# Layer-norm tiles moved to ScalarE in stages, and one set of weight sums moved behind a product's outputs, in a fused attention and gated-MLP kernel

## Chip, cores and metric

The kernel runs on one core of one Trainium2 chip. The metric is the device time of one execution in microseconds (us). A run is given as the median of several executions; the profile is of one execution, and its span is some 2 us shorter than its time (779.9 against 781.72 us for the kernel before).

Engine names: TensorE (PE in the profile; its weight loads are PEld), VectorE (DVE), ScalarE (ACT), GpSimd (POOL), SyncE (SP), which issues most of the DMAs here.

## The reference, cut to what matters

```python
def _layernorm(x, axis=-1, eps=1e-5):
    m = jnp.mean(x, axis=axis, keepdims=True)
    v = jnp.var(x, axis=axis, keepdims=True)
    return (x - m) / jnp.sqrt(v + eps)
...
    h = x + _A_ref(_layernorm(x, axis=-1), A_wqkv, A_wo)     # local dilated attention, 32 heads, window 8
    h2 = h + _B_ref(_layernorm(h, axis=-1), B_w_gate, B_w_up, B_w_down)   # (x Wg * x Wu) Wd
    return h2
```

x is 2048 rows of 1024 numbers in bfloat16. There are two layer norms, one ahead of attention ("first") and one ahead of the MLP ("second").

## The kernel before

The 2048 rows are done in four chunks of 512, each of four tiles of 128 rows. A normalized tile is transposed by a DMA into `lnT`, the moving operand of the next product. Each engine is given its instructions in the order in which the Python code emits them, and in the traces it runs them in that order: in the kernel before, VectorE stood 4.44 us before a weight sum (L661) although the emptying of a bank, emitted behind it (L792), could have run (the products in both banks of `ex` were done by about 505.3, the sum began at 510.42). A bank is one of the eight buffers that the kernel's pool `psum` holds (`bufs=8`), into which TensorE writes its products; the program has another engine empty it (evict the product) before TensorE uses it again, and TensorE waits for that: 3.2 us for L792 on the page of before.

Attention is VectorE work. A small scheduler, `Background`, emits its pieces between TensorE's product groups. Each group gives VectorE a credit of time and each piece takes from it:

```python
    def step(self, us):                 # called once per product group, GROUP_US = 1.73
        self.now += us
        self.credit = min(self.credit + us * self.rate, 4.0)
        while self.credit > 0:
            item = next((i for i in self.items if i[0] <= self.now), None)
            ...
                got = next(item[1])     # emits one piece, returns its estimated time
            ...
```

The output projection of a chunk with its second layer norm, and what follows it for chunk 0:

```python
    def wo_ln2(c):
        ...
        def norm(t):
            ln = normalize(hs[t], mv4, rs4, t)                     # VectorE
            nc.sync.dma_start_transpose(lnT[:, :, bass.ts(t, 128)], ln[:])
        for t in range(4):
            for hf in range(2):
                ... # 8 matmuls, then VectorE adds the product to hs[t]
                if hf == 1:
                    stats(hs[t], mv4, t)                           # VectorE
                    rstd_of(mv4, rs4, t, t + 1)                    # ScalarE, two tiny ones
                    bg.spend(1.5)
                elif t > 0:
                    norm(t - 1)
                    bg.spend(0.55)
                bg.spend(0.7)
                bg.step(GROUP_US)
        norm(3)
        retire(2)              # frees two weight tiles, SyncE issues the next two loads of 1 MB
        return lnT, hs
...
    nxt = wo_ln2(0)                      # product groups 0 to 7
    qkv(3, range(4, 6), last=True)       # product groups 8 to 15; each block of 4 frees a weight tile
    start_attention(3)
    lnT2, hs = nxt
    hT = ffn1(0, lnT2)                   # its first gate product reads all four tiles of lnT
```

Much later, the outputs of a product of chunk 1, with the weight sums of the next stage's first pair in between (a pair is a slice of the gate and up weights that is worked on together; that stage multiplies sums of blocks of the weights and of the normalized rows, here `weight_sums` and `activation_sums`):

```python
    sub([dn["kx"], dn["vx"]], dn["21"], dn["11"])
    weight_sums(0, nc.vector)            # waits for ScalarE's scaled weights, then 4 sums on VectorE
    retire(2)
    for q in range(2):
        dprod(ex[q], q, EF["21"], fcells(dn["12"]), False)
        ... result(1, hs1[2 + q], 2 + q, 1, ex[q], dn["inv"], et)   # VectorE empties bank ex[q]
    retire(1)
    activation_sums(l2, l3, dn["px"])
    for q in range(2):
        dprod(ey[q], q, EF["12"], fcells(dn["22"]), False)
        ...
    for q in range(2):
        dprod(ex[q], q, EF["22"], fcells([dn["kx"], dn["vx"]]), False)  # needs bank ex[q] empty
        ...
```

## Time and profile before

| | |
|---|---|
| time, median (lowest to highest of 4) | 784.56 us (784.07 to 785.24) |
| the profiled execution | 781.72 us, span 779.9 us |
| TensorE busy | 766.8 us |
| VectorE busy | 614.9 us |
| ScalarE busy | 473.5 us |

How to read it: TensorE is busy 766.8 of 779.9 us, at a mean granted clock of 0.999, and its instructions are in program order, so what can be won is its idle time. The busy time of the others counts where TensorE waits for them, as in the 3.2 us for VectorE's L792. The lines follow in the prediction.

### The profile page before, as it was taken

The numbers are of one execution on the slowest core, as the hardware profiler recorded it, in microseconds if no ns is written. First come the engines' busy times: TensorE is split into PE (matmuls) and PEld (weight loads), VectorE is DVE, ScalarE is ACT, GpSimd is POOL, SyncE is SP. The second block draws the span as 40 slices with busy tenths as digits, with TensorE's granted clock in tenths as the row PEclk, the third lists the DMA queues.
The fourth block names the chain that finished last, engine by engine and source line by source line (L and its number), as shares of the span: only waits on it lengthen the run. The fifth ranks groups of instructions, "written<-read, shape, count | busy, mean of one in ns | idle before, by whom it ended". The sixth has DMA issues, their size and how long they took to land.

```text
span 779.9 us, 10436 instructions
## 1 busy us (share of the span) xinstructions
PE 766.8 (98%) x3648; PEld 355.0 (46%) x3707; DVE 614.9 (79%) x805; ACT 473.5 (61%) x1028; POOL 142.4 (18%) x152
## 2 busy tenths in 40 slices
PE   8999999999999999999999999989999999999997
PEld 6544444444444444444444444434444444444444
DVE  6629999999899998999979989975553444579862
ACT  5627445313576652966769799836677677788240
POOL 0000000010000200002000001008778677600000
PEclk9999999999999999999999999999999999999999
DMA  8999693896955868858555492824332323730001
GB/s 272 260 236 209 169 274 90 262 274 173 341 174 186 297 215 234 270 189 270 195 163 195 133 313 75 183 74 110 106 99 64 108 67 97 255 123 28 1 27 55
DMA packets 181605, 133.86 MB, mean 172 GB/s; under 512 B 79024, under 2 KB 174384, under 8 KB 179504
## 3 DMA queue, kind: packets, MB, share of 16 engines
q1 hardware_dynamic: 177968, 111.17, 50.1%
q0 software_dynamic: 3584, 22.02, 8.1%
q8 instruction: 29, 0.48, 0.3%
q14 instruction: 24, 0.20, 0.1%
HBM read 104.86 MB, written 22.02 MB: 163 GB/s over the span
## 4 chain that ended last, share of the span: by engine, by line
PE 88%; DVE 9%; ACT 1%; issue 1%; DMA 1%; SPq 0%; DVEq 0%
PE ps L392 20%; PE pu L392 12%; PE pg L392 12%; PE dx L787 6%; PE pz L680 6%; PE acc L626 6%; PE py L680 6%; PE px L680 6%; PE wo L513 4%; PE pv L680 3%; PE dy L787 3%; DVE h L834 1%; PE ps L355 1%; PE ex L787 1%; DVE prodx L780 1%
## 5 line engine op out<-in xcount | busy, mean ns | idle before, releaser
L392 PE MATMUL ps<-lnT,w_qkv 128*128 128x512 bf16 x721 | 158.9, 379 | 0.8
L392 PEld LDWEIGHTS <-w_qkv 128*128 128x128 bf16 x736 | 71.9, 98 | 85.9
L392 PE MATMUL pu<-lnT,w_wu 128*128 128x512 bf16 x438 | 105.1, 379 | 0.6
L392 PE MATMUL pg<-lnT,w_wg 128*128 128x512 bf16 x440 | 105.1, 379 | 0.4
L306 ACT CAST sg<-ps 128x512 bf16<-128x512 f32 x96 | 54.8, 590 | 54.4 <-PE ps L392 51.1
L475 DVE TENSOR_TENSOR pv<-vD,at 128x4096 bf16<-128x4096 bf16 x32 | 72.5, 2287 | 0.3
L432 DVE TENSOR_TENSOR prod<-qD,kD 128x4096 bf16<-128x4096 bf16 x32 | 72.3, 2284 | 0.1
L680 PEld LDWEIGHTS <-sw 128*128 128x128 f16 x448 | 43.8, 98 | 53.2 <-issue 0.4
L392 PEld LDWEIGHTS <-w_wg 128*128 128x128 bf16 x448 | 43.8, 98 | 52.9
L392 PEld LDWEIGHTS <-w_wu 128*128 128x128 bf16 x448 | 43.8, 98 | 52.9
L596 ACT CAST us<-pu 128x512 bf16<-128x512 f32 x56 | 33.2, 593 | 41.1 <-PE pu L392 38.7
L680 PE MATMUL px<-lnT,ws 128*128 128x512 bf16 x212 | 53.1, 379 | 0.6
L680 PEld LDWEIGHTS <-ws 128*128 128x128 f16 x336 | 32.9, 98 | 39.6
L626 PE MATMUL acc<-w_wd,gs 128*128 128x512 bf16 x219 | 48.2, 379 | 0.3
L487 POOL DMA_DIRECT2D od<-oD x4 | 2.2, 544 | 252.3 <-DVE oD L485 162.5
L661 POOL TENSOR_TENSOR sw<-ws 128x512 f16<-128x512 f16 x26 | 30.0, 1154 | 87.6 <-PE py L680 80.4
L591 ACT CAST gs<-pg 128x512 bf16<-128x512 f32 x56 | 32.9, 587 | 11.4 <-PE pg L392 9.3
L185 ACT ACTIVATE rs<-mv,eps 128x1 f32<-128x1 f32 (+1 forms) x25 | 7.4, 297 | 50.3 <-DVE mv L182 47.1
L434 DVE TENSOR_TENSOR prod<-prod 128x4096 bf16<-128x4096 bf16 x16 | 36.6, 2288 | 0.3
L541 ACT ACTIVATE junkd<-w_wd 128x512 bf16<-128x512 bf16 x56 | 34.3, 613 | 0.0
L626 PEld LDWEIGHTS <-gs 128*128 128x128 bf16 x224 | 21.9, 98 | 26.4
L697 ACT COPY py<-px 128x512 f32<-128x512 f32 x28 | 16.0, 570 | 29.6 <-PE px L680 29.6
(304 smaller groups left out, 1398.0 us busy)
## 6 DMA issues: line engine op xcount, KB each, us to landing
w_wg<-in_B_w_gate_dram SPq DMA_DIRECT2D x14, 1024.0 KB, 6.6
w_wu<-in_B_w_up_dram SPq DMA_DIRECT2D x14, 1024.0 KB, 5.3
w_wd<-in_B_w_down_dram SPq DMA_DIRECT2D x8, 896.0 KB, 7.4
w_pair<-in_B_w_gate_dram SPq DMA_DIRECT2D x14, 512.0 KB, 4.0
w_pair<-in_B_w_up_dram SPq DMA_DIRECT2D x14, 512.0 KB, 5.2
w_wo<-in_A_wo_dram SPq DMA_DIRECT2D x6, 1024.0 KB, 8.4
w_qkv<-in_A_wqkv_dram SPq DMA_DIRECT2D x5, 1024.0 KB, 9.1
kd<-sg SPq DMA_DIRECT2D x32, 144.0 KB, 2.9
```

The lines of the kernel that those rows point to most:

```text
L306: nc.scalar.copy(sg[:, HB:HB + TC], ps[:])
L392: nc.tensor.matmul(ps[:], lhsT=wt[:, ko, bass.ts(j, 128)], rhs=rhs[:, ko, :], start=(ko == 0), stop=(ko == KO - 1))
L432: nc.vector.tensor_tensor(prod[:, j], qD[:], kD[:, :, o:o + SUB], ALU.mult)
L434: nc.vector.tensor_tensor(prod[:, :, 0:16], prod[:, :, 0:16], prod[:, :, 16:32], ALU.add)
L475: nc.vector.tensor_tensor(pv[:, j], vD[:, :, o:o + SUB], at[:, w, None, :].to_broadcast((128, DH, SUB)), ALU.mult)
L513: nc.tensor.matmul(ps[:], lhsT=oTs[c][:, kk, t, :], rhs=wts["wo", c, hf][:, kk, :], start=(kk == 0), stop=(kk == KO - 1))
L541: nc.scalar.activation(junk, src, ACTF.Abs, accum_out=self.l1[:, k:k + 1])
L591: nc.scalar.copy(gs[:], pg[:])
L596: nc.scalar.copy(us[:], pu[:])
L626: nc.tensor.matmul(acc[t][:], lhsT=hT[f][:, bass.ts(t, 128)], rhs=wts["wd", c, hf, b][:, j, :], start=(f == 0), stop=(f == NF - 1))
L680: nc.tensor.matmul(ps[:], lhsT=lhs[:, ko, :], rhs=rhs[:, ko, :], start=(fresh and ko == 0), stop=(ko == 3), skip_group_check=not fresh)
L787: nc.tensor.matmul(ps[:, bass.ds(lo, n)], lhsT=lhs[k][:, bass.ts(q, 128)], rhs=rhs[k][:, bass.ds(lo, n)], start=(fresh and k == 0), stop=( ...
```

## The change

Its intent: VectorE looks full in the first half of the program (busy 19.05 of the 20 us from 180 to 200), so twelve layer-norm tiles are taken from it and done on ScalarE alone, in three stages per tile, one stage per product group. Less important: the absolute sums of the down weights are taken two blocks at a time, and pair 0's weight sums go behind the outputs that they held up.

```diff
     def step(self, us):
         self.now += us
+        if self.rows:
+            next(self.rows[0], None) is None and self.rows.pop(0)
...
+    def scalar_rows(src, lnT, t, name):
+        ...
+        nc.scalar.activation(junk[:], src[:], ACTF.Copy, accum_out=total)
+        yield True
+        nc.scalar.activation(nmean, total, ACTF.Copy, scale=-1.0 / D)
+        ...
+        nc.scalar.activation(junk[:], src[:], ACTF.Square, bias=nmean, accum_out=squares)
+        yield True
+        nc.scalar.activation(rstd, squares, ACTF.Ln, bias=eps[:], scale=1.0 / D)
+        nc.scalar.activation(rstd, rstd, ACTF.Exp, scale=-0.5)
+        nc.scalar.activation(shift, nmean, ACTF.Copy, scale=rstd)
+        ...
+        nc.scalar.activation(ln[:], src[:], ACTF.Identity, bias=shift, scale=rstd)
+        nc.sync.dma_start_transpose(lnT[:, :, bass.ts(t, 128)], ln[:])
+        yield True
...
                 if hf == 1:
-                    stats(hs[t], mv4, t)
-                    rstd_of(mv4, rs4, t, t + 1)
-                    bg.spend(1.5)
-                elif t > 0:
-                    norm(t - 1)
-                    bg.spend(0.55)
+                    bg.rows.append(scalar_rows(hs[t], lnT, t, f"2_{c}_{t}"))
                 bg.spend(0.7)
                 bg.step(GROUP_US)
-        norm(3)
         retire(2)
...
-    bg.add(norm_gen(norm1[3]), bg.now, first=True)
+    bg.rows += [scalar_rows(xtiles[3][t], lnTs[3], t, f"1_3_{t}") for t in range(4)]
...
     lnT2, hs = nxt
+    bg.finish_rows()
     hT = ffn1(0, lnT2)
...
-                if c == 0:
+                if c == 0 and j % 2 == 0:
                     abs_sum_down(hf, b, j)
...
     sub([dn["kx"], dn["vx"]], dn["21"], dn["11"])
-    weight_sums(0, nc.vector)
...
     activation_sums(l2, l3, dn["px"])
+    weight_sums(0, nc.vector)
```

More of the change, by code (lines that the diff above doesn't have):

```diff
@@ L45, in __init__ @@
         self.rate = 1.0
+        self.rows = []
     def add(self, gen, ready=0.0, first=False):
@@ L67, in step, with finish_rows @@
                 self.items.remove(item)
+    def finish_rows(self):
+        for gen in self.rows:
+            for _ in gen:
+                pass
+        self.rows = []
     def finish(self, gen):
@@ L206 @@
     lnTs = {}
+    def scalar_rows(src, lnT, t, name):
+        sm = small.tile([128, 5], F32, tag="am", name="am" + name)
+        total, nmean, squares, rstd, shift = (sm[:, i:i + 1] for i in range(5))
+        junk = lnp.tile([128, D], BF, tag="ln", name="jm" + name)
+        nc.scalar.activation(junk[:], src[:], ACTF.Copy, accum_out=total)
+        yield True
+        nc.scalar.activation(nmean, total, ACTF.Copy, scale=-1.0 / D)
+        junk = lnp.tile([128, D], BF, tag="ln", name="jv" + name)
+        nc.scalar.activation(junk[:], src[:], ACTF.Square, bias=nmean, accum_out=squares)
[3 more added lines that the diff above has]
+        nc.scalar.activation(shift, nmean, ACTF.Copy, scale=rstd)
+        ln = lnp.tile([128, D], BF, tag="ln", name="ln" + name)
+        nc.scalar.activation(ln[:], src[:], ACTF.Identity, bias=shift, scale=rstd)
+        nc.sync.dma_start_transpose(lnT[:, :, bass.ts(t, 128)], ln[:])
+        yield True
     xtiles = {}
@@ L252, in rows_gen @@
                 yield 0.45
-    def stats_gen(n):
-        for t in range(4):
-            n.stat(t)
-            yield 1.5
-    def norm_gen(n):
-        for t in range(4):
-            n.norm(t)
-            n.transpose(t)
-            yield 0.55
     x0 = [hp.tile([128, D], BF, tag="h", name=f"x0_{t}") for t in range(4)]
@@ L381 @@
     xtiles[2] = load_x(2, "x", nc.sync)
-    norm1 = {c: Norm1(c) for c in (1, 2, 3)}
+    norm1 = {c: Norm1(c) for c in (1, 2)}
     bg.add(rows_gen(norm1[1], True))
@@ L502, in wo_ln2 @@
         hs = hss[c]
-        mv4, rs4 = ln_tiles(f"2_{c}")
-        def norm(t):
-            ln = normalize(hs[t], mv4, rs4, t)
-            nc.sync.dma_start_transpose(lnT[:, :, bass.ts(t, 128)], ln[:])
         for t in range(4):
@@ L560, in total @@
             self.s, self.inv = sb[:].bitcast(F32), ib[:].bitcast(F32)
-    scale_gu, scale_d, scale_h = Scale("gu", 56), Scale("d", 56), Scale("h", 56)
+    scale_gu, scale_d, scale_h = Scale("gu", 56), Scale("d", 32), Scale("h", 56)
     scale_h1 = Scale("h1", 28)
@@ L570, in abs_sum_down @@
     def abs_sum_down(hf, b, j):
-        junk = lnp.tile([128, 512], BF, tag="ln", name=f"junkd{hf}_{b}_{j}")
-        scale_d.add(28 * hf + 7 * b + j, wts["wd", 0, hf, b][:, j, :], junk[:])
+        n = min(2, 7 - j)
+        junk = lnp.tile([128, n, 512], BF, tag="ln", name=f"junkd{hf}_{b}_{j}")
+        scale_d.add(16 * hf + 4 * b + j // 2, wts["wd", 0, hf, b][:, j:j + n, :], junk[:])
     def abs_sum_h(n, k, ht):
@@ L735 @@
     pump(6)
-    bg.add(stats_gen(norm1[3]), bg.now + 6.0)
     start_attention(0)
@@ L740 @@
     load_v(0)
-    bg.add(norm_gen(norm1[3]), bg.now, first=True)
+    lnTs[3] = lnTp.tile([128, KO, TC], BF, tag="lnT", name="lnT1_3")
+    bg.rows += [scalar_rows(xtiles[3][t], lnTs[3], t, f"1_3_{t}") for t in range(4)]
     qkv(1, range(4, 6))
@@ L760 @@
     lnT2, hs = nxt
+    bg.finish_rows()
     def f16(ap):
```

## The prediction

The sum at the end of the forecast came to 792.6 us. One of its terms, for matmuls that run slower after so long a wait, rested on no trace and is cut, there and in rival (a); the terms that are left add up to 790.9 (rival (a): 787.6). "Cold clock", and "goes cold" in an expectation below, are words for such slow matmuls: the trace of the kernel before did not show them (its 3.18 us gap left the granted clock at 1.00). The paragraph ahead of "Part 1": 1.06, 1.15 and 1.24 in it are us for 1024 columns, and "both" means bias and scale from pointers.

> **What bounds the kernel now.** I read the page first, then the busy time by stretches of 20 us, then who waited for whom on TensorE (PE), then the timeline of the three places that the change touches.
>
> ```profile
> PE 766.8 (98%) x3648; PEld 355.0 (46%) x3707; DVE 614.9 (79%) x805; ACT 473.5 (61%) x1028; POOL 142.4 (18%) x152
> ...
> 180.00:200.00 20.00, 19.89 (x93) 9.00 (x94) 19.05 (x23) 6.50 (x21) 1.08 (x2) 1.00 0.80 217
> ...
> 500.00:520.00 20.00, 16.82 (x79) 7.58 (x78) 15.24 (x26) 9.68 (x8) 0.00 (x0) 1.00 0.60 119
> ...
> PE ex L787 <- DVE h L792: 3.2, 1, 3.2
> ```
>
> The columns of the two stretches are length, then busy time of PE, weight load, VectorE (DVE), ScalarE (ACT) and GpSimd, then the granted clock. TensorE is busy 766.8 of 779.9 us, so 13.1 us are idle. A full stretch shows 19.89 of 20. Only three stretches fall clearly below that: the start (17.57), the end (15.97) and 500 to 520 (16.82). The change touches neither the start nor the end. So at most about 3.3 us can be won, in one place, and any new wait of TensorE is lost time in full.
>
> The one gap, from the timeline:
>
> ```profile
> 503.96 2.02 DVE L780 TENSOR_TENSOR vx<-w_dn,w_dn 128x3584 f16<-128x3584 f16 x1
> ...
> 506.69 3.69 ACT L654 ACTIVATE ws<-w_pair,sbgu 128x4096 f16<-128x4096 bf16 x1
> ...
> 510.42 0.69 DVE L661 TENSOR_TENSOR sw<-ws 128x1024 f16<-128x1024 f16 x1 [4.44 <-ACT ws L654]
> ...
> 513.75 0.75 DVE L792 SCALAR_TENSOR_TENSOR h<-ex,inv_h1d,et 128x512 bf16<-128x512 f32 x1
> ...
> 514.56 1.67 PE L787 MATMUL ex<-kx,gs 128*128 128x512 f16 x7 [3.18 <-DVE h L792]
> ```
>
> Columns: start, duration, engine, line; in brackets the idle time before it and who ended it. VectorE stood 4.44 us before the weight sums of pair 0 (L661), waiting for ScalarE's scaled weights, then did the four sums. Only then did it empty bank ex[0], for which TensorE had stood since 511.38.
>
> The layer norms, at the change-over from qkv to the first gate product:
>
> ```profile
> 185.85 0.55 DVE L190 TENSOR_SCALAR ln<-h,mv,rs 128x1024 bf16<-128x1024 bf16 x1 [0.60 <-ACT rs L186]
> ...
> 191.13 1.89 PE L392 MATMUL pg<-lnT,w_wg 128*128 128x512 bf16 x8
> 191.33 0.59 ACT L306 CAST sg<-ps 128x512 bf16<-128x512 f32 x1 [1.04 <-PE ps L392]
> 191.81 0.21 ACT L309 COPY sg<-halo 128x16 bf16<-128x16 bf16 x1
> ```
>
> The last tile of chunk 0's second norm is normalized by 186.4. Its transpose (3.1 us from issue to landing here) lands around 190, and the first gate product starts at 191.13 without a wait. The slack is only about a microsecond.
>
> [...] 1.06 (L850, a Copy with a sum), 1.15 (L857, Square with a bias) and 1.24 (L869, Identity with both). [...] ScalarE stood 9.6 us at an exponential (L452), and evictions queued up behind such waits follow each other at 0.58 us. [...] the 3.18 us gap left the granted clock at 1.00.
>
> **Part 1, the norm tiles.** A tile on VectorE costs two statistics and an aggregate (1.45 us) and the normalization (0.55), 2.0 in all. Twelve tiles take 24 us off VectorE, which held nobody up there, so this wins nothing by itself. On ScalarE a tile becomes three stages. Stage 1: Copy with sum, 1.06 + 0.19 for reading the accumulator, about 1.2. Stage 2: a small Copy and Square with sum, about 1.5. Stage 3: Ln 0.30, Exp 0.20, a small Copy 0.20 and Identity 1.24, about 1.95. That is 4.65 per tile, 56 us for twelve tiles against 12 × 0.5 = 6 us of small instructions removed. With the saving of part 2 ScalarE then holds about 515 of 780 us and is not the bound.
>
> What decides is when a stage enters ScalarE's queue: one call per product group. A tile needs **four** calls, because the call that finds the generator ended is also spent. Number the groups from the output projection of chunk 0: 0 to 7 are that projection, 8 to 15 are qkv of chunk 3, blocks 4 and 5. Tile t is queued at group 2t+1. So tile 0 gets its stages after groups 1 to 3 (4 drops it), tile 1 after 5 to 7, tile 2 after 9 to 11 and **tile 3 after 13, 14 and 15**. Group 15 is the last before the gate product, which reads all four tiles. Stage 3 of tile 3 stands behind group 15's own eviction, and TensorE has nothing else to do. The later call that finishes leftovers finds nothing left.
>
> Floor of this wait: group 15 ends at 191.13, eviction and halo until 192.0, stage 3 until 193.95, transpose landed at 197.05. That is **5.9 us** of TensorE.
>
> Is ScalarE on time? Chunk 1's exponential stands in the same queue. I replayed the credit counting on paper. Before, it comes after the first gate group; with the norms no longer spending VectorE credit, it comes after group 10, ahead of tile 3. It needs VectorE's maxima. VectorE's lead: before, it stood until 53.85 for chunk 3's x and began attention at 59.47. The keys land at about 51.3 (issued 42.47, 8.8 to land), so it now starts 8 us earlier, and 1.9 us of normalizations also go: 10 us ahead. It then reaches the first addition at about 164.3 rather than 172.99, and follows TensorE. Adding up its items from 165.4 (eight additions of 0.65, products 2.28 each, tree sums, maxima 2.6), the maxima end at about 186.7. ScalarE from there: exponential 1.06, five evictions at 0.58 (2.9), stage 3 of tile 2 (1.95), stages of tile 3 (1.2 + 1.5 + 1.95), together 10.6, so 197.3. Plus 3.1 is 200.4: a wait of **9.2 us**. [...]
>
> Chunk 1's second norm ends within the 56 steps of the down product, far ahead of its use. Chunk 3's first norm is spread over 16 of 32 groups and used over 20 us later. ScalarE falls at most some 6 us behind there, against eight banks of 1.73 us. Neither costs anything.
>
> **Part 2, sums of the down weights, two at a time.** 56 × (0.61 + 0.19) = 45 us become 24 × (1.06 + 0.19) + 8 × 0.8 = 36 us. This makes room for two norm tiles (9.3) in a stage of 48 us. TensorE doesn't wait for it: 0.
>
> **Part 3, the pair sums moved back.** VectorE then empties ex[0] and ex[1] from 506 on and the 3.18 us gap goes. The activation sums need the last transpose (issued 507.7, 3.3 to land: 511.0) and take until 515.7, the weight sums until 518.3, and two results with their additions (2.9) until 521.2; the next result frees a bank at 521.9. The second pv product of pair 0, at 524.37 before with 0.16 us of waiting for that result, can start at about 522.0. Gain **2.4 us** of the 3.3.
>
> Sum: 784.1 − 2.4 + 9.2[...] = **792.6 us**.
>
> **Rivals.** (a) ScalarE is on time: wait 5.9, [...]gain 2.4: 789.3. For it: only a few microseconds of lag in my sum, which rests on VectorE's place. (b) No new wait, because something holds group 15 or releases the gate earlier: 781 to 782. Against it: the gate's matmuls read all 512 columns, and program order fixes the rest. (c) A transfer in the way of the last transpose: in the second batch of transposes one took 6.3 us instead of 3.3, so 3 more, 795.6. Against it: the 2 MB of q and k loads, issued at 194.67 before, now come about 19 us earlier. (d) ScalarE becomes the bound in the down product and weights come late: a few microseconds, up to 797. Against it: weights are loaded some six tiles ahead.
>
> **Range and chances.** The floor with no cold clock and the full gain of 3.3 is 786.7; (c) or (d) on top of my sum gives 797. I take 786 to 798. Faster by 2% would need 768, more than all gaps together: 0.01. Slower by 2% needs 799.8, i.e. wait and cold clock of 18 us: 0.07. Within 2%: 0.92.
>
> **What would show it.** The first gate product (L392, pg) should show an idle time of 6 to 10 us released by the transposes to lnT; ScalarE's Identity of tile 3 should come after the last qkv eviction; the stretch there should show slower matmuls after the gap. The 3.18 us at ex should be gone, with a smaller wait for L792 at the pair's second product. VectorE's busy time should fall by about 24 us and ScalarE's rise by about 41. I am wrong if the gate product starts without a wait: then the time is about 781.

## The result, and the profile after

The changed kernel takes 795.34 us (median of 4, 794.70 to 795.62) against 784.56 us before. The ratio is 1.0136 (95% interval 1.0118 to 1.0153). Ratios here are the mean time of one kernel's fast runs over that of the other's of the same rounds, so they are not quite the ratio of the medians. That is clearly slower, by 10.8 us.

The busy times on the page of the changed kernel:

```profile
PE 770.4 (97%) x3648; PEld 355.9 (45%) x3707; DVE 593.7 (75%) x757; ACT 516.8 (65%) x1064; POOL 142.2 (18%) x152
```

Who waited on TensorE there (engine, tile and line, then what it waited for: us in total, times, longest):

```profile
PE pg L409 <- DMA lnT<-ln: 12.7, 1, 12.7
...
PE pv L686 <- DVE h L801: 0.9, 2, 0.7
```

VectorE lost 21 us of work and ScalarE gained 43. TensorE waits once for 12.7 us, at the first gate product of chunk 0, for a transpose into lnT. The wait of 3.2 us for L792 is gone; 0.9 us at the first pair's pv products stands in its place.

Three of the 20 us stretches of the changed kernel, with the columns named in the prediction:

```profile
180.00:200.00 20.00, 11.81 (x54) 5.19 (x53) 15.26 (x16) 14.46 (x35) 0.00 (x0) 0.92 1.10 292
200.00:220.00 20.00, 15.41 (x58) 6.46 (x60) 6.71 (x6) 7.00 (x13) 0.00 (x0) 0.74 0.41 95
...
520.00:540.00 20.00, 19.02 (x88) 8.48 (x87) 17.45 (x21) 9.62 (x9) 0.00 (x0) 1.00 0.44 101
```

The loss is all between 180 and 220: TensorE is idle for 12.7 us, and the granted clock is 0.92 in the first stretch and 0.74 in the second. No other stretch loses more than the kernel before.

The timeline of the changed kernel around that wait (start, duration, engine, line, operation; SPq is SyncE's queue of DMA issues; ACT L469 is chunk 1's attention exponential, ACT L232 the last step of a norm tile; a line with xN runs from the start of the first to the end of the last of N, with any waits between them):

```profile
179.85 0.53 SPq L176 DMA_DIRECT2D w_wu<-in_B_w_up_dram  x1
...
180.48 4.61 SPq L176 DMA_DIRECT2D w_wg<-in_B_w_gate_dram  x1
...
185.18 7.34 SPq L336 DMA_DIRECT2D vd<-sg  x4
...
187.49 1.06 ACT L469 ACTIVATE lg<-lg 128x1024 f32<-128x1024 f32 x1 [2.16 <-DVE lg L468]
...
192.61 2.19 SPq L233 DMA_TRANSPOSE lnT<-ln  x1
...
195.51 3.68 SPq L336 DMA_DIRECT2D vd<-sg  x4
...
196.68 1.24 ACT L232 ACTIVATE ln<-h,am 128x1024 bf16<-128x1024 bf16 x1
199.27 2.65 SPq L233 DMA_TRANSPOSE lnT<-ln  x1
...
204.54 3.57 PE L409 MATMUL pg<-lnT,w_wg 128*128 128x512 bf16 x8 [12.68 <-DMA lnT<-ln]
...
207.91 3.08 PE L409 MATMUL pu<-lnT,w_wu 128*128 128x512 bf16 x8
```

The last qkv group ends at 204.54 − 12.68 = 191.86. ScalarE finishes tile 3 at 197.92. Its transpose is issued at 199.27, 1.35 us later, when SyncE has issued the stores of v that stand ahead of it (until 199.19), and it lands 5.1 us later instead of the 3.1 us of before. Then eight matmuls take 3.57 us, 427 ns from one to the next. In the kernel before the same eight take 1.89, 0.216 us from one to the next (a group of eight every 1.73 us, 191.13 to 192.86). The third group of eight starts at 210.82 in the changed kernel's trace, so the first 16 matmuls take 6.3 us instead of 16 × 0.216 = 3.5: 2.8 us lost.

The end of the new order at pair 0, in the changed kernel:

```profile
527.28 1.23 DVE L678 TENSOR_TENSOR prodx<-lnT,lnT 128x2048 f16<-128x2048 bf16 x1 [2.01 <-DMA out_dram<-h]
527.45 1.67 PE L796 MATMUL ex<-kx,gs 128*128 128x512 f16 x7
...
536.08 1.02 PE L686 MATMUL pv<-prodx,sw 128*128 128x512 f16 x4 [0.70 <-DVE h L801]
```

The ex product (L796, kx) starts without a wait. VectorE now stands 2 us before the activation sums; the profile names an output store, but the sums read the last transposes of chunk 3, whose issue ended at 525.1, and the pv product waits 0.7 us for a bank.

### The profile page after: what moved, and what is told of

It is laid out like the page before. It is cut to its first block, busy times and chain, and to the rows that moved or that the text cites. A ratio compares the mean times of both kernels' runs of the same rounds, so it can differ in the third digit from the quotient of the medians.

```text
span 793.8 us, 10407 instructions
## 1 busy us (share of the span) xinstructions
PE 770.4 (97%) x3648; PEld 355.9 (45%) x3707; DVE 593.7 (75%) x757; ACT 516.8 (65%) x1064; POOL 142.2 (18%) x152
## 4 chain that ended last, share of the span: by engine, by line
PE 86%; DVE 9%; DMA 2%; ACT 1%; issue 1%; SPq 0%; DVEq 0%; ACTq 0%
PE ps L409 19%; PE pg L409 12%; PE pu L409 12%; PE dx L796 6%; PE pz L686 6%; PE acc L632 6%; PE py L686 6%; PE px L686 6%; PE wo L524 3%; PE pv L686 3%; PE dy L796 3%; DVE h L843 1%; PE ps L372 1%; DMA w_qkv<-in_A_wqkv_dram 1%; PE ex L796 1%
## 5 line engine op out<-in xcount | busy, mean ns | idle before, releaser
L409 PE MATMUL pg<-lnT,w_wg 128*128 128x512 bf16 x440 | 106.8, 383 | 13.0 <-DMA lnT<-ln 12.7
L409 PEld LDWEIGHTS <-w_wg 128*128 128x128 bf16 x448 | 44.1, 99 | 66.7 <-DMA vd<-sg 13.1
L603 DVE TENSOR_TENSOR gs<-gs,us 128x512 bf16<-128x512 bf16 x56 | 23.5, 420 | 43.6 <-ACT us L602 43.6
L670 POOL TENSOR_TENSOR sw<-ws,sw 128x512 f16<-128x512 f16 x26 | 30.4, 1169 | 0.0
```

Source lines behind the costliest of these rows:

```text
L409: nc.tensor.matmul(ps[:], lhsT=wt[:, ko, bass.ts(j, 128)], rhs=rhs[:, ko, :], start=(ko == 0), stop=(ko == KO - 1))
L670: eng.tensor_tensor(sw[:, i, 3], a12, sw[:, i, 1], ALU.subtract)
```

## The experiments

All experiments give correct results. "Changed" means the changed kernel. The kernel before was run beside each batch; its median was 782.86 in the first batch, 783.58 in the second, 783.74 in the third and 783.59 for the last run. Across batches I compare ratios.

My theory: the loss is the wait at the first gate product plus the slow matmuls after it, less what the pair sums give back. A first rival: ScalarE's added work costs time all over the program. A later one: what the wait itself consists of.

### Each part alone or undone

**Pair sums alone**, on the kernel before. Edit:

```diff
     sub([dn["kx"], dn["vx"]], dn["21"], dn["11"])
-    weight_sums(0, nc.vector)
...
     activation_sums(l2, l3, dn["px"])
+    weight_sums(0, nc.vector)
```

> The kernel before with part 3 alone (the weight sums of pair 0 moved behind the activation sums). Theory: the 3.2 us gap at the ex products goes, a wait of 0.9 us at the pv products of pair 0 comes, as in the changed kernel: 2.4 us less, about 782. Finer theory: the timed runs of before took 784.1 to 785.2, but its profiled run 781.7; if the 3.2 us gap [...]leaves the array at half clock in most runs, the gain in timed runs is 2.4 plus up to 2.8 (as after the long gap of the changed kernel), about 779.5. Rival: the moved sums hold up the first pair products by as much, no gain, 784.

Measured: 779.86 us, ratio 0.9959 (0.9946 to 0.9971). TensorE's waits in that profile:

```profile
PE pv L680 <- DVE h L792: 1.0, 2, 0.8
```

So about 3.0 us by the medians, more than the 2.4 us that the waits account for (3.2 + 0.2 − 1.0), and between the two forms of the theory. Part 3 is a gain by itself. All five runs had a granted clock of 0.999 or 1.000.

**Everything but the pair sums.** Edit: the same lines the other way, on the changed kernel.

> The changed kernel with part 3 undone. Theory: the gap at ex is back, 2.4 us more than the changed kernel, 797.7 (up to 800 if the array goes cold in that gap too). Rival: with VectorE freed of 24 us of norms the gap doesn't come back, because VectorE reaches the sums earlier: 795. Against it, the wait there is for ScalarE's scaled weights, which hang on TensorE's pace.

Measured: 799.29 us, ratio 1.0203. That is 4 us more than the changed kernel by the medians and 5 by the ratios, and the gap is back at the same size. VectorE's freed time did not close it. What the array does after that gap:

```profile
530.85 2.91 PE L796 MATMUL ex<-kx,gs 128*128 128x512 f16 x7 [3.17 <-DVE h L801]
533.54 2.17 PE L796 MATMUL ex<-vx,gs 128*128 128x512 f16 x7
```

The first seven matmuls take 2.91 us instead of 1.67 and the next seven 2.17: (2.91 − 1.67) + (2.17 − 1.67) = 1.7 us lost after a gap of 3.17 us. In the profile of before, the same gap of 3.18 us cost nothing more (the next seven matmuls took 1.67, the granted clock from 500 to 520 was 1.00). The 36 runs of the kernel before beside these experiments fit this: the 12 with a granted clock of 0.999 or more took 782.4 us in the mean, the 24 with 0.995 to 0.998 took 784.0. So in most runs the gap of before seems to cost more than its length, by about 1.7 us. That fits the 3.0 us that part 3 wins instead of 2.4, and the profiled run of before (granted clock 0.999) being faster than its timed ones.

**Chunk 0's second norm back on VectorE**, the rest of the change kept. Edit, cut:

```diff
-                if hf == 1:
+                if c == 0:
+                    ... # statistics, rstd and norm as in the kernel before
+                elif hf == 1:
                     bg.rows.append(scalar_rows(hs[t], lnT, t, f"2_{c}_{t}"))
```

> The changed kernel with chunk 0's second norm alone back on VectorE as before; chunk 3's first, chunk 1's second norm and parts 2 and 3 stay. Theory: everything lost is the wait of 12.7 us at the first gate product and the 2.8 us of half-clock matmuls after it; both go, 795.3 - 15.5 = 779.8. Rival: part of the loss comes from ScalarE's added work elsewhere (chunk 3's first norm, chunk 1's second): then it stays above 783.

Measured: 780.54 us, ratio 0.9965 (0.9953 to 0.9978), with no wait at the gate product. The rival is out: chunk 3's first norm and chunk 1's second on ScalarE, and the sums two at a time, cost nothing that can be seen. They win nothing either, since this is no faster than the pair sums alone.

**All norms stay on ScalarE, but the stages that are left are emitted at the end of the projection.** Edit:

```diff
                 bg.step(GROUP_US)
+        bg.finish_rows()
         retire(2)
```

> The changed kernel with the stages of chunk 0's and chunk 1's second norm that are left emitted at once at the end of the projection (after group 7), so all on ScalarE still. Theory: what costs is only where the last stages stand in ScalarE's order; tile 3's last stage then runs by about 187 and its transpose lands by about 190 to 192, no wait or under 1 us at the first gate product: 780 to 781. Rival (ScalarE's work itself is too long there): the evictions of the qkv groups stand behind 9 us of norm stages and TensorE waits for banks, or the transposes still land late: 784 or more.

Measured: **779.52 us**, ratio 0.9955 (0.9943 to 0.9968). Its timeline:

```profile
172.93 15.81 SPq L233 DMA_TRANSPOSE lnT<-ln  x4
...
188.83 0.53 SPq L176 DMA_DIRECT2D w_wu<-in_B_w_up_dram  x1
...
190.92 1.89 PE L409 MATMUL pg<-lnT,w_wg 128*128 128x512 bf16 x8
```

The gate product starts without a wait. The same work on the same engine, only placed earlier in the order, is some 15 us faster than the changed kernel. Note the DMA queue too (the 15.81 us hold four issues and the waits for the tiles between them): all four transposes are now issued before the weight loads that `retire(2)` starts, as in the kernel before. So this run moves two orders at once, ScalarE's and SyncE's.

### The slow matmuls

**TensorE kept busy while it waits.** Edit:

```diff
     bg.finish_rows()
+    keep = psum.tile([128, TC], F32, tag="mm", name="keep_ps")
+    for i in range(52):
+        nc.tensor.matmul(keep[:], lhsT=ones[:], rhs=ones[:, 0:1].to_broadcast((128, TC)), start=True, stop=True)
     hT = ffn1(0, lnT2)
```

> The changed kernel with 52 matmuls of no use (ones times ones into a bank that nobody reads, 11.2 us) put between the last qkv group and the first gate product, so that TensorE is busy while it waits. Theory: the last transpose lands at the same time, but the 16 matmuls after it run at 216 ns instead of 427: 2.8 us less, 792.5. Rival, that the slow matmuls there come from something else than the idle array (operands arriving late): 795.3, or more if the idle matmuls delay anything.

Measured: 793.41 us, ratio 1.0124.

```profile
191.94 11.48 PE L764 MATMUL keep_ps<-ones 128*128 128x512 bf16 x51
204.22 1.89 PE L409 MATMUL pg<-lnT,w_wg 128*128 128x512 bf16 x8 [0.80 <-DMA lnT<-ln]
```

The gate product still starts at 204, but its eight matmuls now take 1.89 us. The granted clock is 1.00 in all runs. The time fell by 1.9 us by the medians and not 2.8. These medians are of two batches; by the ratios it is only 0.9 us (1.0124, 1.0103 to 1.0144, against 1.0136), within the noise, so the time alone shows nothing. In this run TensorE's wait at the pv products is 1.8 us instead of 0.9; why was not shown. It is the trace that shows the idle array to be the cause of the slow matmuls: the same 16 matmuls after the same late transpose run at full speed once TensorE was kept busy. Their cost is the 2.8 us read above.

### What the wait of 12.7 us is made of

I had put 5.9 us down to the place in the order and 3.3 us to ScalarE being late, held up by the exponential. These runs take them apart.

**Three calls per tile instead of four.** Edit: the third `yield` gives `None`, which drops the tile at once.

> The changed kernel with a tile done in three calls instead of four (the third call also drops it), so tile 3's stages follow groups 10, 11 and 12 instead of 13, 14 and 15. Theory: three groups earlier in ScalarE's order, but the exponential of chunk 1 still stands ahead of the last two stages (it ran at 187.5 in the changed kernel): from 188.6 two evictions of 0.6, stage 2 of 1.5 and stage 3 of 2.0 give 193.3, then 1.3 in the DMA queue and 3.1 to 5.1 to land: a wait of 6 to 8 us instead of 12.7, and the half clock after it stays: 788.5 to 790.5. Rival, that the place after the last group is all that counts: no wait, 780.

Measured: 795.27 us, ratio 1.0146, a wait of 13.1 us. A miss: tile 3 was normalized by 196.0, but its transpose was issued at 198.5 and took 6.6 us to land. So the fourth call alone is not what the wait hangs on.

**The exponential moved behind tile 3's stages.** Edit:

```diff
                     bg.rows.append(scalar_rows(hs[t], lnT, t, f"2_{c}_{t}"))
+                    bg.spend(2.3 if c == 0 else 0.0)
```

> The changed kernel with 2.3 us of VectorE credit booked for each of chunk 0's norm tiles (only a number in the scheduling; no work is added), which puts chunk 1's attention exponential behind the last stage of tile 3 instead of after group 10, as counted on paper. Theory: ScalarE is then on time for tile 3 and the wait loses the 3.3 us by which its last stage came late: 9.4 us or less (down to 6 if the DMA queue is free too), 789 to 792. Rival, that ScalarE is late from its own norm work: no change, 795.

Measured: 796.38 us, ratio 1.0159, a wait of 12.9 us. A miss again. The timeline shows why:

```profile
185.31 0.53 POOL L430 DMA_DIRECT2D kD<-kd  x1 [0.23 <-DMA w_wu<-in_B_w_up_dram]
...
187.96 7.35 SPq L233 DMA_TRANSPOSE lnT<-ln  x1
...
193.60 1.24 ACT L232 ACTIVATE ln<-h,am 128x1024 bf16<-128x1024 bf16 x1
...
199.82 2.57 SPq L233 DMA_TRANSPOSE lnT<-ln  x1
```

ScalarE was on time, at 194.84, and it did not help: the transpose went out five us later, at 199.82, behind the issue of tile 2's transpose (until 195.31), a weight load and four stores of v (until 199.72). But this edit also moved the 2 MB loads of q and k from 176 to 185, where the transpose of tile 2 took 7.35 us to issue beside them. So it is not a clean test.

**The weight load of block 4 behind the last transpose.** Edit:

```diff
-    qkv(3, range(4, 6), last=True)
+    qkv(3, range(4, 6))
+    retire(2)
```

> The changed kernel with the 1 MB weight load that block 4's release starts (issued at 194.9, landing at about 200.8) put behind the last transpose. Theory: of the 12.7 us, 2.0 are the last transpose landing in 5.1 us instead of 3.1, beside that load, and 0.6 the load's own issue ahead in the same queue: the wait falls to about 10 and the time to about 792.7. Rival, that the small stores of v or something else slow the transpose: 795.

Measured: 791.95 us, ratio 1.0105, a wait of 9.3 us. As expected: the last transpose now lands in 3.1 us and is issued at once. Here ScalarE ends last: tile 3 is finished at 199.04 and the transpose issued at 199.07.

```profile
197.80 1.24 ACT L232 ACTIVATE ln<-h,am 128x1024 bf16<-128x1024 bf16 x1
199.07 1.24 SPq L233 DMA_TRANSPOSE lnT<-ln  x1
...
202.25 3.60 PE L409 MATMUL pg<-lnT,w_wg 128*128 128x512 bf16 x8 [9.26 <-DMA lnT<-ln]
```

In the changed kernel and in this one tile 3 is finished 6.1 us after the last qkv group, so this one load is worth 3.4 of the 12.7 us.

**Both edits**, and **three calls with the late load**:

> Both at once: the exponential behind tile 3's stages (as in the run that didn't help) and the 1 MB load behind the last transpose. What is open: taking ScalarE's lateness away left the wait at 12.9 us, because the transpose then stood 5 us in the DMA-issuing queue; taking the load away left 9.3, because ScalarE's last stage then ended last. Theory of two chains side by side, ScalarE's order and the issuing queue, whose later one counts: with both shortened the wait falls well below either, to 6 to 7.5 us, the time to 788.5 to 790.5. Rival, that the queue alone counts (ScalarE's order does nothing): as with the load alone, 9.3 us and 792.

> Three calls per tile instead of four, and the 1 MB load behind the last transpose. With three calls alone tile 3's last stage ended at 196.0, but its transpose was issued at 198.5 and landed 6.8 us later. Theory of two chains: without the load the transpose goes out at 196 to 197 and lands in 3.1 us: a wait of 7 to 8 us, 789.5 to 791. Rival, queue alone: 9.3 us, 792.

Measured: 792.44 us (ratio 1.0113, wait 9.5) and 791.02 us (ratio 1.0093, wait 10.0, of which part is won back by fewer slow matmuls: the first 16 took 4.9 us, 201.36 to 206.26, instead of 6.3). Neither reached the 6 to 8 us of the theory. In both, ScalarE was done over two us before the transpose went out.

**The exponential held back cleanly**, with the late load; q and k stay at 177 to 178. Edit, on the late-load kernel, with the gate opened just before `ffn1(0, ...)`:

```diff
+        while c == 1 and "gate" not in state:
+            yield 1.7
         nc.scalar.activation(lg[:], lg[:], ACTF.Exp, scale=float(DH) ** -0.5)
```

> The last run. The 1 MB load behind the last transpose, as before, and chunk 1's exponential held back until after group 15, this time by letting its credit lapse and not by shifting VectorE's work: in the two runs that shifted the exponential with 2.3 us of booked credit, the 2 MB loads of q and k moved too, from 176 to 185, and the transpose of tile 2 took 7.4 to 7.7 us to issue beside them, so those runs don't tell ScalarE's part. Here q and k stay at about 176. Theory: with ScalarE on time and the queue clear only the floor of the prediction is left: eviction 0.8, stage 3 1.95, transpose 3.1, a wait of 5.9 to 6.7 us; 788.3 to 789.3. Rival, that the issuing queue alone sets the wait: 9.3 us and 792, as with the load alone.

Measured: 791.58 us, ratio 1.0094 (1.0075 to 1.0112), a wait of 8.7 us.

```profile
193.56 2.19 SPq L233 DMA_TRANSPOSE lnT<-ln  x1
...
194.81 1.24 ACT L232 ACTIVATE ln<-h,am 128x1024 bf16<-128x1024 bf16 x1
195.84 2.24 SPq L336 DMA_DIRECT2D vd<-sg  x4
198.17 1.26 SPq L233 DMA_TRANSPOSE lnT<-ln  x1
...
201.75 3.60 PE L409 MATMUL pg<-lnT,w_wg 128*128 128x512 bf16 x8 [8.69 <-DMA lnT<-ln]
```

Now ScalarE is where the floor has it: the group ended at 193.06 and tile 3 is done 3.0 us later, at 196.05. The transpose goes out 2.1 us after that, behind the stores of v, and lands in 3.5. Holding the exponential back thus saved 0.6 us of the wait and not 3.3 (read from one profile of each; by the ratios it is 0.9 us, and the two intervals overlap). My theory falls in this point: SyncE's queue was not a small addition but a second chain of nearly the same length as ScalarE's.

Why the queue is late can be read, though no run isolates it. Work and DMA traffic during the eight qkv groups ahead of the gate product, some 14 us, before:

```profile
177.30:191.10 13.80, 13.75 (x64) 6.26 (x64) 12.95 (x22) 5.72 (x20) 0.00 (x0) 1.00 0.55 109
```

and in the changed kernel:

```profile
178.00:192.00 14.00, 13.81 (x64) 6.08 (x62) 12.38 (x15) 9.26 (x22) 0.00 (x0) 1.00 1.03 329
```

The last two columns are the busy share of the DMA engines and GB/s. Before, the projection's two weight loads stood behind all four transposes in SyncE's order (issued 187.9). In the changed kernel they stand ahead of tiles 2 and 3 (issued 179.9), and q and k are loaded from 176.4. Beside those transfers the second weight load took 4.61 us to issue (180.48 to 185.09; 0.56 before), and the next issue in SyncE's order began at 185.18. The next four stores of v took 7.34 us; before they took 6.26, not much less, but there they stood behind all four transposes.

### An attempt to do better

The version with the stages emitted early, and the two additions into `p5t` moved ahead of the activation sums, where VectorE stands idle.

> An attempt at a version better than all so far: the changed kernel with the leftover stages emitted at the end of the projection (779.5), and the two residual additions into p5t (0.68 us each) put ahead of the activation sums, where VectorE stands 2.0 us for the last transpose. The results that free the banks of pair 0's pv products then come 0.7 and 1.4 us earlier, so the 1.1 us of waiting there goes: 778.5. Rival: VectorE's idle time there is gone or the pair sums bind the same products instead: 779.5.

Measured: 779.46 us (median of 6, 778.61 to 781.87), ratio 0.9951 (0.9933 to 0.9969). The waits at the pv products are gone from its profile, but the time cannot be told from the 779.52 without it. Inconclusive: it is at most a fraction of a microsecond. The best versions are thus this one, the early stages, and the pair sums alone, all between 779.4 and 779.9 us, 0.4 to 0.5% faster than the kernel before.

## Why the prediction was right, point by point

- **What bounds the kernel**: right. TensorE's idle time accounts for the result, and freeing VectorE won nothing.
- **The count of calls**: right as a count. Tile 3's last stage did come after group 15, and emitting the stages earlier removed the wait wholly. But the fourth call was not decisive: with three calls the wait stayed (13.1 us), because ScalarE still finished tile 3 only 3.8 us after the last group, and the transpose went out 2.5 us later and took 6.6.
- **VectorE's lead and the exponential**: right in size. The first addition came at 166.4 (164.3 predicted), the exponential at 187.5 (186.7) and the end of ScalarE's work for tile 3 at 197.9 (197.3).
- **The wait**: 12.7 us against 9.2. This is the term of the sum that was mis-sized, at the step "Plus 3.1 is 200.4": I let the transpose go out at once and land in 3.1 us. It went out 1.35 us later and took 5.1. I had looked only at the q and k loads, under rival (c), and found them moved out of the way. I had not followed SyncE's own order, where `retire(2)` now puts 2 MB of weights ahead of the last two transposes and block 4's release another 1 MB ahead of the last. With that last load out of the way the wait was 9.3 us, as predicted. So rival (c), a transfer in the way of the last transpose, came true with its 795.6 us, but with another transfer than the one it named. The runs also show that the 3.3 us of ScalarE's lateness were largely hidden beside this second chain: holding the exponential back saved 0.6 us.
- **The slow matmuls**: that they would come was right. Their size was too small in the forecast, where it rested on no trace; measured, 16 matmuls took 6.3 us instead of 3.5, so 2.8 us.
- **The pair sums**: 2.4 us in waits, as predicted (0.9 us is left of 3.4). In timed runs they are worth 3.0, since the old gap seems to leave the array slow in most runs (granted clock below 0.999 in 24 of 36). I took the clock of one profiled run for that of all.
- **The other norms and the sums two at a time**: right, nothing seen. VectorE lost 21 us where 24 were forecast, ScalarE gained 43 where 41 were. One term of stage 3 was too small: the small Copy with a pointer as scale took 0.29 us (L230) against 0.20 (L224) without.
- **The sum**: the spans of the two profiles differ by 13.9 us: 12.7 + 2.8 − 2.5 = 13.0, and some 0.6 us come from the first weights landing later. The medians differ by 10.8 us because the timed runs of before are 2.8 us slower than its profiled one. The slow array after the old gap accounts for about 1.7 of that (784.03 − 782.36 in the runs above); the last microsecond stays open. So part of the agreement is luck: the wait and the slow matmuls were together 4.6 us too small (12.7 + 2.8 = 15.5 against the 10.9 that the forecast of 792.6 had for both), but the sum missed by only 2.7, mainly because I read its terms from a fast profile and added them to the slower timed runs.

## What to carry to other kernels

An engine that looks full is worth relieving only where the engine that sets the time waits for it: VectorE lost 21 us of work here, and with the wait at the gate product gone as well (780.54 and 779.52 us) the kernel was no faster than with the pair sums alone (779.86). When work is moved into a queue in pieces, count at which position the last piece lands and compare it with the first reader; a scheduler that spends an extra call per item shifts that position without any instruction showing it. Then follow the same piece through every queue that it has to pass, the DMA-issuing one included, and check what now stands ahead of it there: with one weight load of 1 MB put behind the last transpose, the wait here fell from 12.7 to 9.3 us.

## What the traces show of gaps and of DMA issue

- After a gap of TensorE of 3.17 us (everything but the pair sums), 14 matmuls took 4.7 us (530.85 to 535.55) instead of 14 × 0.216 = 3.0, while in the profile of before a gap of 3.18 us cost nothing. 24 of 36 runs of the kernel before had a granted clock of 0.995 to 0.998, so the loss seems to be the more frequent case. What decides between the two, no run here shows.
- Beside the loads of q and k one tile's transpose took up to 7.7 us to issue and 10.0 to land (the run with both edits), against 1.2 to 1.7 and 3.0 to 3.2 for the four transposes of chunk 0's second norm in the kernel before. In the changed kernel a weight load took 4.6 us to issue behind other loads, against 0.5 to 0.6 for the same two loads before.
